# Global attention rows over 18 key blocks, fewer warm-up products and an earlier mask in an attention and two-MoE kernel

## The chip, the cores and the metric

The kernel runs on one core of a Trainium2 chip. A time is the device time of one execution in microseconds (us); the time that counts is the median of several executions. The engines are TensorE (PE, with its weight loads shown apart as PEld), VectorE (DVE), ScalarE (ACT), GpSimd (POOL) and SyncE (SP), which here starts the transfers. Results of TensorE go to PSUM, which the kernel uses as eight banks of 128x512 f32.

## The reference, cut to what matters

```python
# B=4 batches, H=8 heads, Sl=512 local and Sg=32 global rows, D=64
k_all = concat([k_g, k_l], axis=2);  v_all = concat([v_g, v_l], axis=2)
out_g = softmax(q_g @ k_all.T / 8) @ v_all          # every global row sees all 544 keys
mask  = abs(pos[:, None] - pos[None, :]) <= 32      # a local row sees a window
s_l   = concat([q_l @ k_g.T / 8, where(mask, q_l @ k_l.T / 8, -1e9)])
out_l = softmax(s_l) @ concat([v_g, v_l])
x = concat([out_g, out_l]) as (B * 544 = 2176 rows, 512)
x = (silu(x @ w_gate) * (x @ w_val)) @ w_out        # 512 -> 1536 -> 512
h = x @ w_in;  out = (max(h, 0) + alpha * min(h, 0)) @ w_out2      # 512 -> 2048 -> 512
```

## The kernel before

Attention works on units. A `Local` unit is one pair of heads of one batch (16 units); a `Global` unit (L541 to L628) holds the 32 global rows of four heads, so 128 rows, of one batch (8 units, numbered (batch, group)). The 512 local keys are cut into blocks of 32. In `qk` a pair's keys stand as 26 blocks: for two neighbouring blocks of local rows the host writes the three blocks they see, and position `pos(i) = 3*(i//2) + i%2` starts the 128-column window of row block i, so that neighbouring windows overlap and some blocks stand twice. The values `v` stand likewise, 128 rows to each of 16 windows.

A Global unit before takes six windows, `GWIN = (1, 4, 13, 15, 7, 10)`, which cover all keys; blocks that turn up a second time are masked by `gm`. Its steps are: `s`, scores of 6x128 = 768 columns in two PSUM banks (512 and 256), one DVE instruction for each bank that adds the mask, scales and takes the extremum, then one ACT exponential over 768 columns with its sum; `t(0)` and `t(1)`, four and two transposes of 128x128 and one copy each to `pt`; `pv`, 24 products (six windows, four heads) that add up in one bank, and two DVE scalings that write the result twice; `to`, a transpose and two ACT copies.

The MoE matrices are split into a high and a low part, three products for each. The first MoE runs during attention: its gate and value products (`g<-xa,w`, `v<-xa,w`, groups of 12) and output products (`acc<-h,w`). All of this up to about 400 us is recorded by `Planner` (L58 to L272) as atoms, each for one engine. `order` (L207) sorts them: of the atoms that can start it takes the one due first, by estimated costs (`price`), and `flush` (L265) issues them in that order, which is why nearly all rows of that time stand under L272. One engine runs its instructions in the order so found.

At the start four Local units u0 to u3 (batch 0) use all eight banks. From then on attention has only banks a0 and a1, taken by turns (`att_bank`, L391), while the others belong to the MoE products. The order of the start is in L1037 to L1073: SP loads the first pair's `qk` in four parts, then the next pair, the local mask `lm`, the first values; meanwhile `heat(HEAT)` (L399) runs 20 products of 128x128 on a tile of zeros in bank g. Until the first keys have landed TensorE has no other work. Names in the rows: `e` is a unit's scores and later its exponentials, `pt` their transposes, `o` the output before its transposes, `xa` the MoE input, `sg` the silu's factor, `dbl` and `raw` weights on their way to their two parts, `yp` storage that lends itself to the fourth pair of batch 0 (its `qk` and `v`).

Of the kernel before, what the change touches and what calls it, by code (L numbers as in the profile page):

```python
# [28 lines left out]
NPOS = 26  # L29
WIN = 32 * NPOS  # L30
QK = WIN + S + G
GWIN = (1, 4, 13, 15, 7, 10)
NG = len(GWIN)
# [24 lines left out]
class Planner:  # L58
# [121 lines left out]
    def order(self):  # L180
        atoms, preds = self.atoms, self.graph()
        N = len(atoms)
        size = [sum(o.cost for o in a) for a in atoms]
        eng = [a[0].eng for a in atoms]
        before = [sorted({j for e in p.values() for j, _ in e}) for p in preds]
        for i, b in enumerate(before):
            assert not b or b[-1] < i
        after = [[] for _ in atoms]
        for i, b in enumerate(before):
            for j in b:  # L190
                after[j].append(i)
# [12 lines left out]
        table, dma = None, 0.0  # L204
        left = [len(b) for b in before]
        done = [None] * N
        ready = {e: {} for e in self.ENGINES}  # L207

        def data(i):
            t, off = 0.0, 0.0  # L210
            for m, o in enumerate(atoms[i]):
                for j, k in preds[i].get(m, ()):
                    x = done[j][k] - off
                    if eng[j] == eng[i]:
                        x -= atoms[j][k].lat if eng[i] != "sync" else 0.0
# [106 lines left out]
def kernel(  # L322
# [59 lines left out]

    yg = const.tile([128, 4, 128], F32, name="yg")
    lm = attc.tile([128, 4, 128], BF16, name="lm")
    gm = attc.tile([128, 64, 1], BF16, name="gm")[:, 0:4 * NG]
    def bank(tag):
        return ps.tile([128, 512], F32, tag=tag, name="ps_" + tag)

# [7 lines left out]
    zero = attc.tile([128, 128], BF16, name="zero")  # L396
    nc.vector.memset(zero, 0.0)

    def heat(n):  # L399
        t = bank("g")  # L400
        with nc.atom():
            for _ in range(n):
                nc.tensor.matmul(out=t[:, 0:128], lhsT=zero, rhs=zero, start=True, stop=True)


    class Pair:
# [134 lines left out]
    class Global(Unit):  # L541
# [2 lines left out]
            self.pairs = [pairs[b][2 * grp + i] for i in range(2)]  # L544

        def s(self):
            self.sg = attp.tile([128, 1024], F32, tag="e", name="sg")[:, 0:128 * NG]
            self.sm = attp.tile([128, 16], F32, tag="sm", name="smg")[:, 0:1]
            mx = attp.tile([128, 16], F32, tag="mx", name="mxg")
            for part, ws in enumerate((GWIN[0:4], GWIN[4:6])):  # L550
                n = 128 * len(ws)
                s = att_bank()
                with nc.atom():
                    for i in range(0, n, 256):
                        w0, w1 = (32 * pos(w) for w in ws[i // 128:i // 128 + 2])
                        for j in range(4):
                            x = self.pairs[j // 2].qk
                            rows = slice(D * (j % 2), D * (j % 2) + D)
                            step = w1 - w0
                            if step >= 128:  # L560
                                srcs = [(x[rows, w0:w0 + 2 * step].rearrange("p (a c) -> p a c", a=2)[:, :, 0:128], 0)]
                            else:
                                srcs = [(x[rows, w0:w0 + 128], 0), (x[rows, w1:w1 + 128], 128)]
                            for r, d in srcs:
                                dst = s[32 * j:32 * j + 32, i + d:i + d + 256 // len(srcs)]
                                nc.tensor.matmul(
                                    out=dst.rearrange("p (a c) -> p a c", c=128) if len(srcs) == 1 else dst,
                                    lhsT=x[rows, WIN + S:QK],
                                    rhs=r,
                                    start=True,  # L570
                                    stop=True,
                                )
                nc.vector.tensor_tensor_reduce(
                    out=self.sg[:, 512 * part:512 * part + n].rearrange("p (b c) -> p b c", c=32),
                    in0=s[:, 0:n].rearrange("p (b c) -> p b c", c=32),
                    in1=gm[:, 16 * part:16 * part + n // 32].to_broadcast([128, n // 32, 32]),
                    scale=-0.125,
                    scalar=3e38,
                    op0=ALU.add,
# [6 lines left out]
            )  # L586

        def t(self, h):
            if h == 0:
                self.pt = attp.tile([128, 1024], F32, tag="pt", name="ptg")  # L590
            t = att_bank()
            c0, c1 = (0, 512) if h == 0 else (512, 128 * NG)
            with nc.atom():
                for i in range(c0, c1, 128):
                    nc.tensor.transpose(t[:, i - c0:i - c0 + 128], self.sg[:, i:i + 128], ident)
            evac(self.pt[:, c0:c1], t[:, 0:c1 - c0], cp())
            if h == 1:
                self.rc = rc = attp.tile([128, 16, 1], F32, tag="rc", name="rcg")[:, 0]
                nc.vector.tensor_scalar(out=rc, in0=self.sm, scalar1=1e-9, scalar2=None, op0=ALU.add)
                nc.vector.reciprocal(out=rc, in_=rc)  # L600

        def pv(self):
            o = att_bank()
            with nc.atom():
                for i, w in enumerate(GWIN):
                    for j in range(4):
                        nc.tensor.matmul(
                            out=o[32 * j:32 * j + 32, 0:D],
                            lhsT=self.pt[:, 128 * i + 32 * j:128 * i + 32 * j + 32],
                            rhs=self.pairs[j // 2].v[:, j % 2, w],  # L610
                            start=(i == 0),
                            stop=(i == NG - 1),
                        )
            rc = self.rc
            self.o = attp.tile([128, 8, D], F32, tag="o", name="og", bufs=1)
            for h in range(2):
                nc.vector.tensor_scalar(
                    out=self.o[:, h], in0=o[:, 0:D], scalar1=rc, scalar2=None, op0=ALU.mult
                )

        def to(self):
            t = att_bank()
# [957 lines left out]
```

## Time and profile before

| what | value |
|---|---|
| device time, median of 3 runs | 884.55 us (884.41 to 884.82) |
| time of the profiled execution | 886.36 us |
| its span, first to last instruction | 884.6 us |
| mean granted TensorE clock | 0.997 |
| busy share of PE, DVE, ACT | 98%, 78%, 60% |

The profiled execution is one of its own, 1.81 us longer than the median. A row of the timeline gives the start and the length of a group of like instructions, then engine, line, operation, `output<-inputs`, shapes, the count, and in brackets the idle time ahead of it on its engine and what ended that. An f32 product of a tile is recorded as two instructions, so that the 16 score products of a Global unit are `x32`.

### The profile page before, as it was taken

Reading aid. Unit: us, or ns where it says so; the run is one execution under the profiler, and the core shown is the slowest. Engines: PE = TensorE matmul, PEld = TensorE weight load, DVE = VectorE, ACT = ScalarE, POOL = GpSimd, SP = SyncE. Lnnn points to the kernel's source line nnn. Section 1 sums busy time; section 2 is a strip of 40 time slices with the busy share of each in tenths; the row PEclk is TensorE's granted clock in tenths of the full one; section 3 lists DMA queues with packets and bytes.
Section 4 is the critical chain, followed back from the end, with each engine's and each line's share of the span. In section 5 each row is a group of like instructions: output and inputs, shape, how many; then the busy total and the mean of one; then the engine's idle time right before and its main releaser. Section 6 shows DMA issues by size and latency. Waiting matters only on the chain.

```text
span 884.6 us, 17317 instructions
## 1 busy us (share of the span) xinstructions
PE 864.1 (98%) x6868; PEld 749.6 (85%) x6868; DVE 690.8 (78%) x1441; ACT 527.2 (60%) x1051; POOL 0.7 (0%) x6
## 2 busy tenths in 40 slices
PE   5899999999999999999999999999999999999997
PEld 4677778888788787778999999889999889999996
DVE  3997989989877856597666687777896777977776
ACT  5899999878686786654333346343545434554442
POOL 0000000000000000000000000000000000000000
PEclk9999999999999999999999999999999999999999
DMA  8799989899969899975566576455474645585631
GB/s 346 290 408 414 359 340 377 328 361 386 405 261 334 293 343 329 371 291 171 167 234 228 202 256 243 167 219 209 171 285 186 245 183 202 227 293 212 280 143 60
DMA packets 41665, 239.30 MB, mean 271 GB/s; under 512 B 4848, under 2 KB 5488, under 8 KB 19312
## 3 DMA queue, kind: packets, MB, share of 16 engines
q1 hardware_dynamic: 41584, 238.19, 71.5%
q8 instruction: 54, 0.88, 0.4%
q14 instruction: 27, 0.22, 0.1%
HBM read 183.38 MB, written 54.79 MB: 269 GB/s over the span
## 4 chain that ended last, share of the span: by engine, by line
PE 88%; DMA 6%; DVE 2%; ACT 2%; issue 1%; SPq 0%; ACTq 0%; DVEq 0%
PE ps_acc L1450 21%; PE acc L272 10%; PE g L272 10%; PE v L272 10%; PE ps_g L1239 9%; PE ps_v L1239 9%; PE ps_a L1239 8%; PE a L272 7%; PE ps_acc L1296 3%; DMA w2so<-dbl 2%; PE ps_a L1296 2%; DMA dbl<-in_w_dram 2%; DMA qk<-in_qk_dram 1%; DMA yp<-in_w_dram 1%; DMA hring<-w1ss1v 1%
## 5 line engine op out<-in xcount | busy, mean ns | idle before, releaser
L1450 PE MATMUL ps_acc<-w,hring 128*128 128x512 f32 x816 | 194.2, 391 | 0.0
L1450 PEld LDWEIGHTS ps_acc<-w,hring 128*128 128x128 f32 x816 | 152.1, 188 | 30.0 <-ACT hring L1419 0.3
L272 PE MATMUL g<-xa,w 128*128 128x512 f32 x432 | 107.5, 397 | 3.0 <-ACT sg L272 2.2
L272 PE MATMUL v<-xa,w 128*128 128x512 f32 x432 | 106.9, 396 | 0.0
L272 PE MATMUL acc<-h,w 128*128 128x512 f32 x432 | 106.1, 394 | 0.0
L1414 ACT ACTIVATE r<-c 128x384 f32<-128x384 f32 (+1 forms) x96 | 47.8, 498 | 93.2 <-DVE c L1247 93.2
L1455 DVE TENSOR_TENSOR oacc<-ps_acc,oacc 128x512 f32<-128x512 f32 x119 | 81.8, 690 | 22.0 <-PE ps_acc L1450 20.7
L272 PEld LDWEIGHTS g<-xa,w 128*128 128x128 f32 x432 | 79.1, 188 | 22.4 <-ACT sg L272 3.3
L272 PEld LDWEIGHTS acc<-h,w 128*128 128x128 f32 x432 | 79.8, 188 | 18.6 <-issue 1.8
L272 PEld LDWEIGHTS v<-xa,w 128*128 128x128 f32 x432 | 79.3, 188 | 18.3 <-issue 1.4
L1419 ACT ACTIVATE hring<-g 128x384 fp32r<-128x384 f32 (+1 forms) x96 | 48.6, 506 | 55.8 <-DVE g L1416 55.5
L1420 DVE TENSOR_TENSOR hring<-g,hring 128x384 fp32r<-128x384 f32 (+1 forms) x96 | 51.1, 532 | 18.9 <-ACT hring L1419 16.1
L272 ACT ACTIVATE e<-e,mx 128x128 f32<-128x128 f32 (+1 forms) x136 | 57.2, 423 | 13.7 <-DVE mx L272 13.5
L1416 DVE SCALAR_TENSOR_TENSOR g<-g,nal,r 128x384 f32<-128x384 f32 (+1 forms) x96 | 56.7, 591 | 10.6 <-ACT g L1415 10.0
L272 ACT ACT_TABLE_LOAD x46 | 59.0, 1283 | 5.3 <-PE g L272 3.8
L1415 ACT ACTIVATE g<-c 128x384 f32<-128x384 f32 (+1 forms) x96 | 47.9, 499 | 13.7 <-DVE hring L1420 13.7
L1239 PE MATMUL ps_v<-xa,w 128*128 128x320 f32 (+1 forms) x288 | 53.1, 319 | 0.6 <-ACT p L1255 0.5
L1239 PE MATMUL ps_g<-xa,w 128*128 128x320 f32 (+1 forms) x288 | 53.4, 318 | 0.2
L1239 PE MATMUL ps_a<-w 128*128 128x384 f32 (+1 forms) x288 | 51.4, 326 | 0.0
L1239 PEld LDWEIGHTS ps_v<-xa,w 128*128 128x128 f32 x288 | 46.9, 188 | 2.2 <-ACT p L1255 0.7
L1239 PEld LDWEIGHTS ps_g<-xa,w 128*128 128x128 f32 x288 | 47.1, 188 | 1.9 <-DVE u L1263 0.4
L1239 PEld LDWEIGHTS ps_a<-w 128*128 128x128 f32 x288 | 47.9, 188 | 0.1
(209 smaller groups left out, 1397.7 us busy)
## 6 DMA issues: line engine op xcount, KB each, us to landing
dbl<-in_w_dram SPq DMA_DIRECT2D x28, 1024.0 KB, 7.6
w<-w2so SPq DMA_DIRECT2D x24, 1024.0 KB, 5.8
w<-w2sx SPq DMA_DIRECT2D x24, 1024.0 KB, 4.8
w<-w2ss SPq DMA_DIRECT2D x24, 1024.0 KB, 6.6
v<-in_v_dram SPq DMA_DIRECT2D x15, 1024.0 KB, 10.8
qk<-in_qk_dram SPq DMA_DIRECT2D x14, 688.0 KB, 9.5
w2sx<-dbl SPq DMA_DIRECT2D x8, 1024.0 KB, 6.8
w2so<-dbl SPq DMA_DIRECT2D x8, 1024.0 KB, 8.7
```

Source lines behind the costliest of these rows:

```text
L272: last[o.eng] = getattr(getattr(self.nc, o.eng), o.op)(*o.args, **o.kw)
L1239: nc.tensor.matmul(out=o[:, 0:n], lhsT=left(name, a, k), rhs=x[name][:, b, k, 0:n], start=(i == 0), stop=(i == 5),)
L1296: mm = nc.tensor.matmul(out=o, lhsT=a, rhs=x, start=(first and e == 0 and not second), stop=((j, f, e) == (NF1 // 2 - 1, 0, 2) and i not i ...
L1414: nc.scalar.activation(out=rr, in_=u, func=ACTF.Relu)
L1415: nc.scalar.activation(out=g, in_=u, func=ACTF.Relu, scale=-1.0)
L1416: nc.vector.scalar_tensor_tensor(out=g, in0=g, scalar=nal[:, i:i + 1], in1=rr, op0=ALU.mult, op1=ALU.add)
L1419: nc.scalar.activation(out=hi, in_=g, func=ACTF.Copy)
L1420: nc.vector.tensor_tensor(out=lo, in0=g, in1=hi, op=ALU.subtract)
L1450: nc.tensor.matmul(out=o, lhsT=a, rhs=x, start=(i == 0), stop=(i == 5))
L1455: nc.vector.tensor_tensor(out=oacc[tb], in0=o, in1=oacc[tb], op=ALU.add)
```

## The change

The global rows take each key block once. Of the 26 positions, the first two of each group of three hold 16 different blocks (`x[rows, 0:768]` seen as 8 groups of 96, of each the first 64 columns), and the last two positions hold the remaining two: 18 blocks, 576 columns, in parts of 512 and 64. Scores are one product for each head and part, 8 instead of 16. The transposes of a unit go from six to five: four as before, and one over columns 448 to 576, of which the lower 64 rows are copied. The value product cannot use whole windows any more, since a pair of blocks is either the upper or the lower 64 rows of a window: it is done in two halves, even groups on rows 0 to 63 (16 products) and odd groups on rows 64 to 127 (20 products), each in its own bank, taken by `att_bank`; one scaling of the first bank and one scale-and-add of the second put them together. `HEAT` goes from 20 to 4. The second part of the first pair and the mask `lm` are one atom, and `order` now prices each transfer of a SyncE atom for itself.

```diff
-    SLACK=60.0, LOOK=0.1, SWITCH=4.0, MARGIN=0.5, HEAT=20, ND=3, NR=3, LAG=6,
+    SLACK=60.0, LOOK=0.1, SWITCH=4.0, MARGIN=0.5, HEAT=4, TINY=0, ND=3, NR=3, LAG=6,
+GHALF = [(4 * (g // 2) + g % 2, g % 2) for g in range(8)] + [(NB - 2, 1)]
+GLAST = 32 * (pos(NB - 2) + 2)
...
             if e == "sync":
-                dma = max(dma, y + 0.3) + atoms[i][0].lat
-                done[i] = [dma + 1.9]
-                y += 0.45
+                for o in atoms[i]:
+                    dma = max(dma, y + 0.3) + o.lat
+                    done[i].append(dma + 1.9)
+                    y += o.cost
...
-            for part, ws in enumerate((GWIN[0:4], GWIN[4:6])):
+            for part, (c0, n) in enumerate(((0, 512), (512, 64))):
                 s = att_bank()
                 with nc.atom():
+                    for j in range(4):
+                        x = self.pairs[j // 2].qk
+                        rows = slice(D * (j % 2), D * (j % 2) + D)
+                        if part:
+                            dst, r = s[32 * j:32 * j + 32, 0:64], x[rows, GLAST:GLAST + 64]
+                        else:
+                            dst = s[32 * j:32 * j + 32, 0:512].rearrange("p (a c) -> p a c", c=64)
+                            r = x[rows, 0:96 * 8].rearrange("p (a c) -> p a c", a=8)[:, :, 0:64]
+                        nc.tensor.matmul(out=dst, lhsT=x[rows, WIN + S:QK], rhs=r, start=True, stop=True)
...
+                nc.tensor.transpose(t[:, 0:128], self.sg[:, 448:576], ident)
+                evac(self.pt[D:2 * D, 512:640], t[D:2 * D, 0:128], cp())
...
         def pv(self):
+            for half in range(2):
+                o = att_bank()
+                parts.append(o)
+                rows = slice(D * half, D * half + D)
+                mine = [(g, w) for g, (w, k) in enumerate(GHALF) if k == half]
+                with nc.atom():
+                    for i, (g, w) in enumerate(mine):
+                        c = 128 * (g // 2)
+                        for j in range(4):
+                            nc.tensor.matmul(
+                                out=o[32 * j:32 * j + 32, 0:D],
+                                lhsT=self.pt[rows, c + 32 * j:c + 32 * j + 32],
+                                rhs=self.pairs[j // 2].v[rows, j % 2, w],
...
+            nc.vector.tensor_scalar(out=part[:, 0], in0=parts[0][:, 0:D], scalar1=rc, scalar2=None, op0=ALU.mult)
+            nc.vector.scalar_tensor_tensor(
+                out=self.o[:, 0:2],
+                in0=parts[1][:, 0:D].rearrange("p (a d) -> p a d", a=1).to_broadcast([128, 2, D]),
...
-        heat(HEAT)
-        nc.sync.dma_start(out=lm, in_=lmask)
-        p0[0].load_qk(1)
+        heat(HEAT, 128)
+        heat(P["TINY"], 32)
+        with nc.atom():
+            p0[0].load_qk(1)
+            nc.sync.dma_start(out=lm, in_=lmask)
         p0[1].load_qk()
```

What moves with it shows in the order of three stretches. On SP at the start, before (`qk_100` is the first pair, 448 and 256 columns its first part, 384 and 288 its second; `qk_101` the second pair):

```order
L272 DMA qk_100<-in_qk_dram 128x448
L272 DMA qk_100<-in_qk_dram 128x384
L272 DMA qk_100<-in_qk_dram 128x288
L272 DMA qk_100<-in_qk_dram 128x256
L272 DMA qk_101<-in_qk_dram 128x1376
L272 DMA lm<-in_lmask_dram 128x512
L272 DMA v_108<-in_v_dram 128x2048
```

and after:

```order
L276 DMA qk_100<-in_qk_dram 128x384
L276 DMA qk_100<-in_qk_dram 128x288
L276 DMA lm<-in_lmask_dram 128x512
L276 DMA qk_100<-in_qk_dram 128x448
L276 DMA qk_100<-in_qk_dram 128x256
L276 DMA qk_101<-in_qk_dram 128x1376
L276 DMA v_108<-in_v_dram 128x2048
```

The mask has moved ahead of the first part of the first pair, whose last transfer is now fifth instead of fourth.

On PE behind the scores of u3 (`acc<-yp_94`, the last of the four Local units of the start), after:

```order
L276 MATMUL acc_126<-yp_94 32x128
L276 MATMUL acc_125<-yp_94 32x128
L276 MATMUL acc_121<-ident,o_130 128x128 x4
L276 MATMUL acc_122<-ident,e_116 128x128 x4
L276 MATMUL a_114<-ident,e_115 128x128 x4
L276 MATMUL v_129<-ident,e_115 128x128 x4
L276 MATMUL g_103<-v_109,pt_124 32x64 x32
L276 MATMUL acc_126<-ident,e_116 128x128 x4
L276 MATMUL a_114<-qk_100 32x64 x2
L276 MATMUL a_114<-qk_101 32x64 x2
L276 MATMUL a_113<-ident,o_130 128x128 x4
```

The rows down to the value product `g_103<-v_109,pt_124` stand in the same order before; the scores behind are Global(0,0)'s, whose short part of 64 columns now goes first, its long part seven rows later.

On PE at the value product of Global(0,1) (`v_110` and `yp_93` are the two pairs' values), before:

```order
L272 MATMUL a_114<-ident,o_130 128x128
L272 MATMUL a_113<-v_110,pt_124 32x64 x2
L272 MATMUL a_113<-yp_93,pt_124 32x64 x2
...
L272 MATMUL a_113<-v_110,pt_124 32x64 x2
L272 MATMUL a_113<-yp_93,pt_124 32x64 x2
L272 MATMUL g_103<-xa,w_137 128x512 x12
L272 MATMUL a_114<-qk_100 32x256 x2
L272 MATMUL a_114<-qk_101 32x256 x2
```

and after:

```order
L276 MATMUL a_113<-ident,o_130 128x128
L276 MATMUL a_114<-v_110,pt_124 32x64 x2
L276 MATMUL a_114<-yp_93,pt_124 32x64 x2
...
L276 MATMUL g_103<-xa,w_137 128x512 x12
L276 MATMUL a_113<-v_110,pt_124 32x64 x2
L276 MATMUL a_113<-yp_93,pt_124 32x64 x2
...
L276 MATMUL a_114<-qk_100 32x512 x2
L276 MATMUL a_114<-qk_101 32x512 x2
L276 MATMUL v_129<-xa,w_137 128x512 x12
L276 MATMUL a_113<-qk_100 32x64 x2
L276 MATMUL a_113<-qk_101 32x64 x2
```

The two halves of the value product stand 12 MoE products apart, the second runs straight into the next unit's long scores, and the short scores stand another 12 products later.

## Rows read from the trace of the kernel before

**Rows 1.** The page, busy time, share of the span and instructions of each engine.
```profile
PE 864.1 (98%) x6868; PEld 749.6 (85%) x6868; DVE 690.8 (78%) x1441; ACT 527.2 (60%) x1051; POOL 0.7 (0%) x6
```

**Rows 2.** Windows: stretch, its length, busy by engine, PEclk, DMA share, GB/s.
```profile
0.00:50.00 50.00, 36.82 (x698) 28.97 (x698) 33.28 (x111) 35.04 (x92) 0.70 (x6) 0.97 0.86 330
50.00:100.00 50.00, 49.37 (x578) 39.05 (x577) 43.33 (x106) 49.68 (x93) 0.00 (x0) 1.00 0.99 395
100.00:150.00 50.00, 49.97 (x661) 39.55 (x661) 46.41 (x111) 49.59 (x105) 0.00 (x0) 1.00 0.93 371
```

**Rows 3.** Waits of PE: us in total, times, the longest.
```profile
PE g L272 <- ACT sg L272: 2.2, 2, 1.3
PE a L272 <- ACT pt L272: 1.0, 2, 0.6
```

**Rows 4.** Timeline of the first 10 us, SP, PE and DVE.
```profile
0.74 2.30 SPq L272 DMA_DIRECT2D qk<-in_qk_dram  x5
0.99 2.32 PE L272 MATMUL g<-zero 128*128 128x128 bf16 x20 [0.99 <-DVE zero L272]
7.77 1.96 PE L272 MATMUL a<-qk 64*32 64x128 f32 x64 [4.47 <-DMA qk<-in_qk_dram]
9.83 0.29 DVE L272 CUSTOM_DVE_ANT_0 e<-a,lm 128x128 f32<-128x128 f32 x1 [8.90 <-PE a L272]
```

**Rows 5.** Timeline around 21 to 23 us, PE, DVE and ACT.
```profile
21.45 0.41 PE L272 MATMUL acc<-yp 64*32 64x128 f32 x3 [3.46 <-issue]
21.89 0.29 DVE L272 CUSTOM_DVE_ANT_0 e<-acc,lm 128x128 f32<-128x128 f32 x1 [4.13 <-PE acc L272]
23.13 0.40 ACT L272 ACTIVATE e<-e,mx 128x128 f32<-128x128 f32 x1 [1.55 <-DVE mx L272]
```

**Rows 6.** The page, a DMA queue: kind, packets, MB, share.
```profile
q8 instruction: 54, 0.88, 0.4%
```

**Rows 7.** The same queue between 17.9 and 21.4 us.
```profile
q8 instruction: 1, 0.02, 1.8%
```

**Rows 8.** Windows: the stretch of 3 us behind that gap.
```profile
22.50:25.50 3.00, 3.00 (x40) 2.67 (x42) 2.97 (x17) 2.37 (x13) 0.00 (x0) 0.50 1.00 418
```

**Rows 9.** Instruction groups by form, DVE on Global scores: busy, mean ns.
```profile
L272 DVE CUSTOM_DVE_ANT_1 e<-a,gm 128x512 f32<-128x512 f32 x8 | 5.5, 684 | 1.6 <-PE a L272 1.6
L272 DVE CUSTOM_DVE_ANT_1 e<-a,gm 128x256 f32<-128x256 f32 x8 | 3.4, 424 | 0.0
```

**Rows 10.** Timeline of PE, runs of score, value, transpose and MoE products.
```profile
46.70 0.82 PE L272 MATMUL a<-ident,e 128*128 128x128 f32 x6
...
61.06 0.88 PE L272 MATMUL a<-v,pt 128*32 128x64 f32 x48
...
71.55 1.03 PE L272 MATMUL a<-ident,e 128*128 128x128 f32 x8
...
79.13 1.54 PE L272 MATMUL a<-qk 64*32 64x256 f32 x32
80.60 1.65 PE L272 MATMUL v<-xa,w 128*128 128x512 f32 x6
...
87.28 1.10 PE L272 MATMUL a<-v,pt 128*32 128x64 f32 x64
...
91.26 1.16 PE L272 MATMUL a<-qk 64*32 64x128 f32 x64
...
153.98 2.88 PE L272 MATMUL acc<-h,w 128*128 128x512 f32 x12
156.70 2.88 PE L272 MATMUL g<-xa,w 128*128 128x512 f32 x12
...
285.78 1.11 PE L272 MATMUL a<-qk 64*32 64x256 f32 x24
286.82 3.03 PE L272 MATMUL acc<-h,w 128*128 128x512 f32 x12
289.78 0.64 PE L272 MATMUL a<-qk 64*32 64x256 f32 x8
```

More of the change, by code (lines that the diff above doesn't have):

```diff
@@ L31 @@
 QK = WIN + S + G
-GWIN = (1, 4, 13, 15, 7, 10)
-NG = len(GWIN)
+NGB = NB + 2
 P = dict(
-    SLACK=60.0, LOOK=0.1, SWITCH=4.0, MARGIN=0.5, HEAT=20, ND=3, NR=3, LAG=6,
+    SLACK=60.0, LOOK=0.1, SWITCH=4.0, MARGIN=0.5, HEAT=4, TINY=0, ND=3, NR=3, LAG=6,
     wr0=0.75, wr2=0.5, wr3=0.75, wr4=0.6, wr5=0.2,
@@ L384 @@
     lm = attc.tile([128, 4, 128], BF16, name="lm")
-    gm = attc.tile([128, 64, 1], BF16, name="gm")[:, 0:4 * NG]
+    gm = attc.tile([128, 64, 1], BF16, name="gm")[:, 0:NGB]
     def bank(tag):
@@ L397, with heat @@
     nc.vector.memset(zero, 0.0)
-    def heat(n):
+    def heat(n, cols):
         t = bank("g")
@@ L402, in heat @@
             for _ in range(n):
-                nc.tensor.matmul(out=t[:, 0:128], lhsT=zero, rhs=zero, start=True, stop=True)
+                nc.tensor.matmul(
+                    out=t[0:cols, 0:cols], lhsT=zero[:, 0:cols], rhs=zero[:, 0:cols], start=True, stop=True
+                )
     class Pair:
@@ L546, in s @@
         def s(self):
-            self.sg = attp.tile([128, 1024], F32, tag="e", name="sg")[:, 0:128 * NG]
+            self.sg = attp.tile([128, 1024], F32, tag="e", name="sg")[:, 0:32 * NGB]
             self.sm = attp.tile([128, 16], F32, tag="sm", name="smg")[:, 0:1]
             mx = attp.tile([128, 16], F32, tag="mx", name="mxg")
-            for part, ws in enumerate((GWIN[0:4], GWIN[4:6])):
-                n = 128 * len(ws)
+            for part, (c0, n) in enumerate(((0, 512), (512, 64))):
@@ L552, in s @@
                 s = att_bank()
                 with nc.atom():
[L554 to L572, printed above, removed]
@@ L573, in s @@
                 nc.vector.tensor_tensor_reduce(
-                    out=self.sg[:, 512 * part:512 * part + n].rearrange("p (b c) -> p b c", c=32),
+                    out=self.sg[:, c0:c0 + n].rearrange("p (b c) -> p b c", c=32),
                     in0=s[:, 0:n].rearrange("p (b c) -> p b c", c=32),
-                    in1=gm[:, 16 * part:16 * part + n // 32].to_broadcast([128, n // 32, 32]),
+                    in1=gm[:, c0 // 32:(c0 + n) // 32].to_broadcast([128, n // 32, 32]),
                     scale=-0.125,
@@ L591, in t @@
             t = att_bank()
[L592 to L597, printed above, removed]
+            if h == 0:
+                with nc.atom():
+                    for i in range(0, 512, 128):
+                        nc.tensor.transpose(t[:, i:i + 128], self.sg[:, i:i + 128], ident)
+                evac(self.pt[:, 0:512], t, cp())
+            else:
+                nc.tensor.transpose(t[:, 0:128], self.sg[:, 448:576], ident)
+                evac(self.pt[D:2 * D, 512:640], t[D:2 * D, 0:128], cp())
                 self.rc = rc = attp.tile([128, 16, 1], F32, tag="rc", name="rcg")[:, 0]
@@ L602, in pv @@
         def pv(self):
[L603 to L613, printed above, removed]
+            parts = []
+            for half in range(2):
[7 more added lines that the diff above has]
+                        for j in range(4):
+                            nc.tensor.matmul(
+                                out=o[32 * j:32 * j + 32, 0:D],
+                                lhsT=self.pt[rows, c + 32 * j:c + 32 * j + 32],
+                                rhs=self.pairs[j // 2].v[rows, j % 2, w],
+                                start=(i == 0),
+                                stop=(i == len(mine) - 1),
+                            )
             rc = self.rc
             self.o = attp.tile([128, 8, D], F32, tag="o", name="og", bufs=1)
[L616 to L619, printed above, removed]
+            part = self.o[:, 2:3]
+            nc.vector.tensor_scalar(out=part[:, 0], in0=parts[0][:, 0:D], scalar1=rc, scalar2=None, op0=ALU.mult)
+            nc.vector.scalar_tensor_tensor(
+                out=self.o[:, 0:2],
+                in0=parts[1][:, 0:D].rearrange("p (a d) -> p a d", a=1).to_broadcast([128, 2, D]),
+                scalar=rc,
+                in1=part.to_broadcast([128, 2, D]),
+                op0=ALU.mult,
+                op1=ALU.add,
+            )
         def to(self):
@@ L1039 @@
         p0[0].load_qk(0)
-        heat(HEAT)
-        nc.sync.dma_start(out=lm, in_=lmask)
-        p0[0].load_qk(1)
+        heat(HEAT, 128)
+        heat(P["TINY"], 32)
+        with nc.atom():
+            p0[0].load_qk(1)
+            nc.sync.dma_start(out=lm, in_=lmask)
         p0[1].load_qk()
@@ L1552 @@
             lmask[32 * c:32 * c + 32, t, 32 * j:32 * j + 32] = np.where(ok, 0.0, NEG)
-    seen, gm = set(), []
-    for w in GWIN:
-        for b in blocks[pos(w):pos(w) + 4]:
-            gm.append(NEG if b[0] == "x" or b in seen else 0.0)
-            seen.add(b)
-    gmask = np.broadcast_to(np.array(gm, np.float32), (128, 4 * NG))
+    gm = [NEG if b[0] == "x" else 0.0 for g in range(8) for b in blocks[3 * g:3 * g + 2]] + [0.0, 0.0]
+    gmask = np.broadcast_to(np.array(gm, np.float32), (128, NGB))
     arrays = {
```

## The prediction

> **What bounds the kernel now.** I read the page's busy shares first, then windows of 50 us, PE's waits, the timeline of the head, and last the runs of PE instructions by which the changed groups are priced. PE is busy 98% of the span [rows 1]. By stretches it is busy 36.82 of the first 50 us, 49.37 of the next and 49.97 of the third [rows 2]: behind about 45 us the time is PE's own work, and only ahead of that is there something to wait for. So an edit counts in full on PE behind 45 us, counts on the path through DMA, DVE and ACT ahead of it, and counts nothing on DVE or ACT later, where PE's work covers it (behind 45 us PE waits for ACT's `sg` and `pt` once each, 0.9 and 0.4 us, the sums of [rows 3] less the longest).
>
> The head, in order: SP starts the first five transfers in 2.30 us, PE does 20 warm-up products from 0.99 for 2.32 us, then stands still 4.47 us until the first pair has landed, and at 7.77 begins u0's scores; DVE's first masked score follows at 9.83, released by PE and not by the mask [rows 4]. Then PE has a gap of 3.46 us up to 21.45 that no semaphore explains ("issue"). It falls three records ahead of the end of u3's scores. DVE, which needs these, is idle 4.13 us, and ACT, next in the chain, 1.55 us [rows 5]. In this gap lies one packet of the queue that carries instructions [rows 7]. There are 54 such packets in all [rows 6], for 2 x 6868 = 13736 products and weight loads on PE [rows 1], 254 for each. I read the gap as PE running out of fetched instructions while the transfers take 418 GB/s right behind it [rows 8].
>
> **The change part by part.** I sum against the profiled execution, 886.36 us (span 884.6 and 1.76 around it), 1.81 above the median of 884.55. A forecast is 886.36 + change - 1.81.
>
> *Head.* (1) The mask now goes ahead of the last part that u0 waits for: at least its 128 KB, 0.31 us at 418 GB/s [rows 8], at most one start of 2.30 / 5 = 0.46 us [rows 4]. I take 0.35, near the bytes, since what follows already queues. The mask itself gains nothing, as DVE waited for PE. (2) 16 warm-up products and their loads go, 32 instructions. The products ran in the 4.47 us wait, so their own time is free. But if a packet holds a fixed number, the fetch gap falls 32 instructions later in the program: behind u3's scores and some 13 of the 16 transposes that stand ahead of `g_103<-v_109,pt_124`. DVE then gets u3's scores without the gap and ACT's 1.55 us go. That ACT is what the head follows there I take from its run without a break up to the gap. Bounds: nothing to 3.46 us; I take 1.55, since behind the chain ACT is next in line. (3) Global score work on DVE: 512 columns 0.684, 256 columns 0.424 [rows 9], so 64 columns 0.424 - 192 x 0.260 / 256 = 0.229, 0.195 less for each of the two units of the head, 0.39. (4) The copy behind `t(1)` shrinks from 256 columns on 128 rows to 128 on 64, and I let the 0.64 us go that PE waits for `pt` [rows 3]. Later units save as much on DVE and ACT, which PE's work hides; without that cover it would be some 0.2 to 0.5 us for a unit. Head: 0.35 - 1.55 - 0.39 - 0.64 = -2.23 us. Bounds: +0.35 when nothing comes of (2) to (4), -5.0 when the PE waits of 3.46, 1.26 and 0.64 all go.
>
> *PE, eight units.* Busy rows of [rows 10]: scores of 256, 512 and 768 columns take 0.64, 1.11 and 1.54 us; by a line between them 576 take 1.22 and 64 some 0.29. An extra run costs more than its row: the 12 MoE products between two short runs take 289.78 - 286.82 = 2.96 us, elsewhere 156.70 - 153.98 = 2.72, and a run's row reaches 0.07 past the next start (79.13 + 1.54 against 80.60), so 0.17 net. Value products: 24 take 0.88 and 32 take 1.10, 0.0275 each; 16 take 0.66, 20 take 0.77, 36 in one run 1.21. These have half the rows (K = 64), a form no row shows: bounds for the 36 are 1.10, if a product on 64 rows is cheaper than one on 128 by a tenth, and 1.21; the Local scores on 64 rows, 1.16 for 32 products, speak for no large gain, so I take 1.15, the middle.
> - Scores: units (0,0) and (3,0) split as before, 1.11 + 0.29 against 1.11 + 0.64: -0.35 each. Contiguous in (0,1), (1,1), (2,1): -0.32 each. Contiguous before, split now in (1,0), (2,0), (3,1): 1.11 + 0.29 + 0.17 - 1.54 = +0.03 each. Sum -1.57. The first units' scores, -0.67, lie in the head where PE waits anyway: -0.90 counts.
> - Value products: in one run in (0,0) and (1,0), +0.27 each. Split by 12 products in six units: 0.66 + 0.77 + 0.17 - 0.88 = +0.72 each, 4.32. Sum +4.86.
> - Three of the second halves run straight into scores, as in the order of Global(0,1), so two runs become one: 0.15 each, -0.45.
> - Transposes: eight take 1.03 and six 0.82, 0.11 for one, eight fewer: -0.88.
>
> Together +2.63 us; bounds by the contiguous pairs and the run price (0.07 to 0.24) some +1.6 to +3.4. The Trainium skill ("TensorEngine Tiling (Array Packing)", Key Properties) says that a change of tiling mode, not of the tile, drains TensorE. The value products go from 128x32 tiles to the 64x32 of the scores, so by that rule the three glued halves change no mode and save a whole run price; the traces show the price of a run as above (0.24 with its surroundings) but not what of it is the mode. By the page the sum would be 3 x 0.09 = 0.27 us lower.
>
> *Sum.* -2.23 + 2.63 = +0.40; 886.36 + 0.40 - 1.81 = **884.95 us**, no change to speak of (0.2%, 1.77 us, is about what a measurement here can tell).
>
> **The rivals.**
> - *B, the head gives back more.* If the gap of 3.46 us disappears behind transfers or the queue of work, and the two waits for ACT (1.26 and 0.64) go with it: 0.35 - 5.36 = -5.01, + 2.63: 882.17 us. For it: the gap is PE's longest wait but one and ACT and DVE stand idle because of it. Against it: ACT has 49.68 busy of 50 us from 50 to 100 [rows 2] and is full from there.
> - *C, the fetch gap comes back on the path, slower.* The gap only moves; where it falls, the transposes and u1's value product feed DVE and ACT just the same. Then nothing of (2) to (4) is gained and the late start stands: +0.35 + 2.63 = +2.98, 887.53 us. It decides when DVE and ACT run dry for 1.55 us or more behind the moved gap. For it: the gap was 3.46 us, and four exponentials of 0.40 us [rows 5] are all that u3 gives ACT for a half. Against it: the work of both halves of u3 is then in front of ACT.
> - *D, the second bank, slower.* The value product needs two of the two banks a0 and a1, and each must have been read out by its last user, the copy of `t(1)` or the scaling. At the mean of PE's waits for `pt`, 1.0 / 2 = 0.5 us [rows 3], in four of the units that have only 12 products (2.72 us) between the halves: +2.0 on the forecast, 886.95. Against it: PE's 12 products are longer than a reading of 512 columns, 0.684 us on DVE [rows 9].
> - *E, the clock.* PE did 20 products ahead of the 4.47 us wait and then did u0's 64 score records in 1.96 us, where the same form takes 1.16 later [rows 4, 10]: what it did before did not keep it at the faster pace. With 4 products the slow stretch could reach to a third group, 0.8 us, and some transposes, 1.0 together: 885.95. The granted clock of 0.50 (1.2 GHz) stands in the trace behind the gap of 3.46 us [rows 8]. By the Trainium skill ("TensorE: Matmul & The Clock Gate", Part 1) the throttled state is the default and activity lifts it, so that taking out warm-up work can only cost; the rows show that at this place there was little to lose.
>
> **How the numbers follow.** Forecast 0.47 (its own range 883.4 to 886.3, from +-0.9 on PE and +-1.2 in the head), B 0.24, C 0.15, D 0.10, E 0.04. Faster by over 0.2% (under 882.78): 0.20 of B and 0.03 of the forecast, 0.23. Slower by over 0.2% (above 886.32): 0.13 of C, 0.07 of D, 0.04 of the forecast and 0.01 of E, 0.25. Within: 0.52. The range goes from 881.9, a little below B's time, to C's, 887.5; the tails past B and C make up the two in ten.
>
> **What would show it.** In the profile after: PE's first scores at 8.0 to 8.3 us; the gap of about 3 us some 26 instructions behind u3's scores, with DVE's idle time before u3's first score gone; PE's waits for `sg` and `pt` before 52 us shorter; at 62 us the same MoE products about 2.2 us earlier than before, at 400 us level or 0.4 us late; the value halves as rows of 0.66 and 0.77 us; 0.29 for the short scores. It is wrong if the gap stands where it stood or a new one of over 1 us appears behind a value half (C, D), if u2's scores take 1.96 us (E), or if PE's idle time before 62 us shrinks by over 4 us (B).

## The result, and the profile after

The changed kernel takes 894.21 us (median of 4 runs, 892.11 to 897.47), the kernel before 884.68 (4 runs, 884.41 to 884.90): ratio 1.011, interval 1.0089 to 1.013. It is 9.5 us slower. The forecast was 884.95, no change to speak of, in a range of 881.9 to 887.5: the measured time lies 6.7 us above that range. The profiled execution took 892.11 us with a span of 890.3, 5.7 us above that of before, and is the fastest of the four; the others granted a lower mean clock (0.992 to 0.993 against 0.996), which is worth at most some 3 us of their time (an estimate: 0.0035 of 893 us). So the two profiles show 5.7 of the 9.5 us.

The page's engine line (answers to [rows 1]) and the windows (answer to [rows 2], the third 50 us; the two of 3.4 us are the stretches at half clock behind 45 us):

```profile
PE 866.1 (97%) x6908; PEld 746.5 (84%) x6908; DVE 688.9 (77%) x1441; ACT 525.0 (59%) x1049; POOL 0.7 (0%) x6
```

```profile
100.00:150.00 50.00, 49.05 (x654) 38.28 (x653) 45.14 (x111) 48.01 (x89) 0.00 (x0) 0.97 0.86 341
117.80:121.20 3.40, 3.40 (x10) 2.62 (x9) 2.32 (x6) 3.37 (x11) 0.00 (x0) 0.50 0.98 296
302.10:305.50 3.40, 3.24 (x68) 2.79 (x68) 1.29 (x2) 3.33 (x6) 0.00 (x0) 0.50 0.82 286
```

DVE and ACT have less to do, as the change intends, and PE's busy time has hardly risen. But PE, which stood still 0.03 us of the third 50 us before, now stands 0.95, and its clock is 0.50 in two stretches of 3.4 us, where before there was none between 26 us and the end. PE's waits from 52 to 420 us (answer to [rows 3]):

```profile
PE a L276 <- ACT pt L276: 3.7, 4, 2.9
PE v L276 <- DVE t L276: 1.0, 1, 1.0
PE a L276 <- ACT y L276: 0.7, 1, 0.7
PE a L276 <- ACT yp L276: 0.7, 1, 0.7
PE acc L276 <- DVE h L276: 0.4, 1, 0.4
```

That is 6.5 us by this list; before, the waits in the same stretch were 1.3. The head, on the other hand, gave back what was forecast. PE's timeline there, and the last row of ACT's `e` ahead of PE's second wait (answers to [rows 4, 5]):

```profile
6.35 1.96 PE L276 MATMUL a<-qk 64*32 64x128 f32 x64 [4.75 <-DMA qk<-in_qk_dram]
...
21.53 0.49 PE L276 MATMUL v<-ident,e 128*128 128x128 f32 x3 [1.80 <-ACT e L276]
...
23.57 0.32 PE L276 MATMUL a<-qk 64*32 64x64 f32 x8
...
27.80 0.48 PE L276 MATMUL acc<-v,pt 128*32 128x64 f32 x20 [1.05 <-issue]
```

```profile
20.96 0.19 ACT L276 ACTIVATION_READ_ACCUMULATOR e<-e,mx 128x1 f32 x1
```

The first scores start 1.42 us earlier than before, not 0.35 later. The first MoE product stands at 32.28 us instead of 34.33; one execution says little here, since in the profiles of the 16 kernels below with the same changes in the head it stands between 31.57 and 34.05. The gap of 3.46 us stands where the prediction moved it: before, PE does 349 products ahead of it, and after, where 16 of them are gone, the 349 end one product into the last four of the 16 transposes, and there PE stands 1.80 us. The view puts this to ACT's `e`, but the last of these ended at 21.15, 0.38 us before PE went on. A further gap of 1.05 us, with no releaser, follows 128 products on. So the gap has not gone, it is shorter; how much of the 1.80 us is the fetch of instructions and how much ACT stays open. Two groups of rows show what came later, PE's timeline at Global(1,0)'s value product, and at the output transpose of Global(2,1) with a Local unit's value product behind it:

```profile
115.31 0.65 PE L276 MATMUL a<-v,pt 64*32 64x64 f32 x32
116.63 0.76 PE L276 MATMUL a<-v,pt 64*32 64x64 f32 x40 [0.67 <-ACT yp L276]
117.32 4.60 PE L276 MATMUL acc<-h,w 128*128 128x512 f32 x12
```

```profile
295.98 2.98 PE L276 MATMUL v<-xa,w 128*128 128x512 f32 x12
301.82 0.33 PE L276 MATMUL a<-ident,o 128*128 128x128 f32 x1 [2.86 <-ACT pt L276]
302.31 1.93 PE L276 MATMUL a<-v,pt 128*32 128x64 f32 x64 [0.16 <-ACT pt L276]
304.22 3.65 PE L276 MATMUL g<-xa,w 128*128 128x512 f32 x12
```

In the first the second half stands 0.67 us for its bank, and the 12 MoE products behind, 2.88 us elsewhere [rows 10], take 4.60 at half clock. In the second PE waits 2.86 us for that Local unit's copies to `pt`. Why ACT is late there stands in ACT's and SP's timelines:

```profile
297.98 1.12 ACT L276 ACTIVATE raw<-dbl 128x1024 f32<-128x1024 f32 x1 [9.46 <-DMA dbl<-in_w_dram]
299.12 1.28 ACT L276 ACT_TABLE_LOAD   x1
300.42 0.77 ACT L276 ACTIVATE e<-e,mx 128x576 f32<-128x576 f32 x1
...
301.19 1.06 ACT L276 ACTIVATE pt<-a 128x512 f32<-128x512 f32 x2
```

```profile
279.81 0.33 SPq L276 DMA_DIRECT2D v<-in_v_dram  x1
280.55 0.32 SPq L276 DMA_DIRECT2D w2so<-dbl  x1
...
288.93 0.33 SPq L276 DMA_DIRECT2D dbl<-in_w_dram  x1
```

ACT stands 9.46 us in front of the first step of a weight conversion, with the exponential of Global(3,0) behind it. The weights were sent for at 288.93, once the store `w2so<-dbl` had emptied the buffer; the store was queued on SP behind a load of `v`, which waited for PE's second half (279.02 to 279.78) of Global(2,1)'s value product to let go of the values. The sum of the profiled executions: head's idle time 13.8 us in both, PE's gaps that end between 52 us and the end of the first MoE 5.5 against 1.3, time lost in the half-clock stretches there 3.3 against none (half of PE's busy time in them), the rest 1.8 less: +5.7 us.

### The profile page after: what moved, and what is told of

Its sections match the earlier page's. It is cut to its first block, busy times and chain, and to the rows that moved or that the text cites. A ratio compares the mean times of both kernels' runs of the same rounds, so it can differ in the third digit from the quotient of the medians.

```text
span 890.3 us, 17376 instructions
## 1 busy us (share of the span) xinstructions
PE 866.1 (97%) x6908; PEld 746.5 (84%) x6908; DVE 688.9 (77%) x1441; ACT 525.0 (59%) x1049; POOL 0.7 (0%) x6
## 4 chain that ended last, share of the span: by engine, by line
PE 73%; DMA 10%; ACT 8%; DVE 6%; issue 1%; SPq 1%; ACTq 0%; DVEq 0%
PE ps_acc L1463 21%; PE ps_g L1252 9%; PE ps_v L1252 9%; PE ps_a L1252 8%; PE acc L276 6%; PE g L276 6%; PE v L276 5%; DMA dbl<-in_w_dram 4%; PE a L276 4%; PE ps_acc L1309 3%; PE ps_a L1309 2%; DMA w2so<-dbl 2%; ACT e L276 1%; ACT L276 1%; DVE y L276 1%
## 5 line engine op out<-in xcount | busy, mean ns | idle before, releaser
L276 PE MATMUL acc<-h,w 128*128 128x512 f32 x432 | 108.1, 400 | 0.4 <-DVE h L276 0.4
L1468 DVE TENSOR_TENSOR oacc<-ps_acc,oacc 128x512 f32<-128x512 f32 x119 | 81.8, 691 | 22.1 <-PE ps_acc L1463 20.9
L1428 ACT ACTIVATE g<-c 128x384 f32<-128x384 f32 (+1 forms) x96 | 47.9, 499 | 13.6 <-DVE hring L1433 13.5
```

The source lines that it names most:

```text
L276: last[o.eng] = getattr(getattr(self.nc, o.eng), o.op)(*o.args, **o.kw)
L1428: nc.scalar.activation(out=g, in_=u, func=ACTF.Relu, scale=-1.0)
L1468: nc.vector.tensor_tensor(out=oacc[tb], in0=o, in1=oacc[tb], op=ALU.add)
```

## The experiments

All were timed beside runs of the kernel before; a time is a median, the ratio is to the kernel before. They form five series (1 to 4, 5 to 8, 9 to 12, g, h), in which the kernel before has medians from 884.25 to 885.57 us, so a difference between two series is better read from the ratios. Where an order is said to be kept, the list of atoms to issue stands in the kernel as a table (`PLAN`) instead of the planner's own:

```diff
-        for i in self.order():
+        for i in PLAN:
```

**1 to 4. Which part, and are six runs the price?**

```diff
 e3: before,      HEAT=20 -> HEAT=4
 e1: before,      HEAT=4, the mask's atom and the planner's pricing as in the change
 e2: the change,  HEAT=20, mask and load_qk(1) as before
 e4: the change,  one nc.atom() around both halves of pv instead of one around each
```

> The head's part of the change alone (4 warm-up products, mask in one atom with the first pair's second part, transfers of an atom priced singly) on the global rows of before. Behind the head its order is that of before nearly row for row. Theory 'order' (the loss of 9.5 us comes from the new order of all engines that the global part brings, by waits on ACT and DVE and the half-clock stretches behind them): this part keeps what the head gives back, 882 to 884 us. Theory 'work' (the loss is the global part's own PE work): the same. Theory 'head' (4 products are too few, or the earlier mask delays): slower than before, 887 us or more.

883.52 us (ratio 0.9985, 0.997 to 0.9999): faster by some 1.2 us, barely clear of no difference. "Head" falls.

> The global rows' part alone, with 20 warm-up products and the mask where it was. Theory 'order': slower than before by the 2.6 us of PE work and by waits of a new order of its own, 888 to 897 us, with PE waits behind 45 us at other places than after the whole change. Theory 'work': slower by the loss after the change and what the head gave there, 9.5 + 2 us, 896 us, with hardly any PE waits behind 45 us. Theory 'head': 887 us or less.

891.99 (1.0081, 1.0057 to 1.0104). The loss is the global part's. With 20 products the fetch gap is back (3.2 us "issue").

> The kernel before with 4 warm-up products instead of 20 and nothing else; the order of all engines is that of before but for the 16 products. If the instruction packets hold a fixed number, the fetch gap (3.46 us at 17.99) moves 32 instructions on, behind u3's scores, and DVE and ACT no longer stand still for u3: 1.5 to 2.5 us less, 882 to 883 us. If the gap stays where it is: 884.6 us. Theory 'head': slower, 886 us or more, with the granted clock back to full later than 12.24 us.

884.15 (0.9993, 0.998 to 1.0007): the gap has moved, as in the change. Behind the same 349 products PE stands 1.66 us, put to ACT's `e`, which had ended 0.94 us before PE went on, and 0.64 us ("issue") 128 products later. What the move gives back is no more than 1.8 us and can't be told from nothing, nor from e1's gain, so that the mask's place is not shown to give anything.

> The changed kernel with the two halves of a value product in one atom, so that they stand together in one run of 36 products. Theory 'work': six runs fewer, about 0.45 us each, 2.7 us less: 891.5 us. Theory 'order': the order of the rest changes again, so that the time follows the PE waits behind 45 us and the half-clock stretches, and not the 2.7 us: anything from 885 to 897 us.

884.99 (1.0013, 0.9991 to 1.0035): 9.2 us less than the change, three times the six runs, so the runs' price is not the cause.

**5 to 8. The order, or the work?**

```diff
 e5: the change,  PLAN = each atom at its counterpart's place in e1's order
 e6: e1's work,   PLAN = each atom at its counterpart's place in the changed kernel's order
 e7: the change,  its own order, one ACT atom (raw<-dbl at 297.98) behind e of Global(3,0) and the two pt copies
 e8: as e5,       each second half behind the next group of 12 MoE products
```

> All of the changed kernel's work, but issued in the order of the kernel before (with the head's part): each atom stands where its counterpart stood, both halves of a value product where the one stood, so in one run. Theory 'order': 883.5 us of the head's part alone, scores -1.6, transposes -0.9, eight value products in one run +0.3 each: about 883.5 us, between 882 and 886. Theory 'work': no better than with the halves in one run in an order of its own, less nothing, and if the halves cost what the changed kernel lost, 889 us or more.

895.47 (1.0119, 1.0099 to 1.014). Against "order".

> The reverse: the work of the kernel before (with the head's part; six windows, six transposes, 24 products), issued in the order of the changed kernel. Theory 'order': it loses most of what the changed kernel lost, 889 to 894 us, with PE waits at the same places (118 us, 300 us). Theory 'work': 883 to 885 us, as with the head's part alone.

884.62 (0.9998, 0.9982 to 1.0014). "Order" falls: the old work in the new order loses nothing. But "work" as PE time doesn't explain e4.

> The changed kernel with one atom moved: ACT's first step of a weight conversion, which waited 9.46 us for its transfer at 297.98 us, stands behind the exponential and the two copies of Global(3,0) instead of ahead of them. Theory 'order': PE's wait of 2.86 us at 301.8 and the half-clock stretch at 302.1 (1.7 us) go, 4 to 5 us less than the changed kernel: 889.5 us. Rival: the conversion is needed as soon, and the wait turns up behind it: 893 to 895 us.

891.16 (1.007, 1.0049 to 1.0091): 3 us less. PE's wait did turn up behind, for `sg`, 3.4 us at 299 us: the rival, in part. The two copies that the expectation gives to Global(3,0) are a Local unit's.

> As the replay of the old order, but in all eight units the second half of the value product stands one MoE group of 12 products behind the first. By the prices of the prediction a split costs 0.45 us: 3.6 us more than the replay, 887 us. Rival 1: MoE products between the halves hide the cost, the same time as the replay. Rival 2: the half-clock stretches come with split halves, 6 us or more above the replay.

889.27 (1.0047, 1.0028 to 1.0065): 6 us less than with the halves in one run, the opposite of every expectation. Contiguous halves wait for something that halves apart don't. The waits name it: in e5 PE waits 5.2 us for ACT's `y` and `yp`, the copies of a unit's output out of the other bank; in e8 0.3.

**9 to 12. The second bank, and the values held.** New theory: what the second half needs, not what it does, costs the time. In e9 and e10 the work and order are e1's, with one thing changed in the value product.

```diff
 e9:  24 products in one run, out = (bank 1 if i < 3 else bank 2), then scale, scale and add
 e10: one bank, windows 0-2 and 3-5 in two atoms, the second behind the next 12 MoE products
 e11: the change, its own order, second half right behind the first
 e12: the change, its own order, on SP each later load of v two transfers further back
```

> The work of the kernel before with the head's part, in that kernel's order (883.5 us), but the 24 products of a global unit's value product, still on 128 rows and in one run, go to two banks, windows 0 to 2 to one and 3 to 5 to the next, and are scaled and added as in the changed kernel. Theory 'second bank' (a unit takes a0 and a1 seven times instead of six, and the value product waits in front for ACT to have read the bank of the transposes just ahead): PE waits on ACT's y and yp as in the replay (5 us, and half-clock stretches behind), 891 to 895 us. Theory 'rows' (products on 64 rows cost the time): 883 to 885 us.

894.36 (1.0116, 1.0074 to 1.0158), with products on 128 rows, old scores, old transposes. PE's waits from 52 to 420 us, then the value product of one unit:

```profile
PE a L335 <- ACT y L335: 4.9, 2, 2.9
PE a L335 <- ACT yp L335: 2.4, 2, 1.5
```

```profile
380.48 0.60 PE L335 MATMUL a<-ident,o 128*128 128x128 f32 x4
381.00 0.54 PE L335 MATMUL a<-v,pt 128*32 128x64 f32 x24
384.49 0.54 PE L335 MATMUL a<-v,pt 128*32 128x64 f32 x24 [2.94 <-ACT y L335]
```

The four transposes of the output fill one bank, the first half the other, and the second half stands 2.94 us until ACT has copied the transposes. "Rows" falls: the second bank alone makes this loss in the old order (10.8 us above e1, 11.6 by the ratios).

> The same order and work, one bank for a value product, but its 24 products in two runs of 12 with one MoE group between them in all eight units. Price of a split by the prediction 0.17 + 0.2 us of busy time, 8 x 0.4 = 3 us, 886.5 us. Theory 'values held' (the split keeps the value tiles in use 3 us longer, SP's load of the next ones waits and all transfers queued behind it): more than that, 888 us or more, with SP waiting longer for PE in front of loads of v. If the split is free: 883.5 us.

889.53 (1.0066, 1.0044 to 1.0088), 6 us above e1: more than the 3 us put on the runs. SP's waits for PE's `a` products from 52 to 420 us go from 22.1 to 37.5 us, as "values held" has it. But of the difference between the two profiles (5.5 us) 1.85 lie ahead of the first MoE product, where no product is split yet, so this run alone does not decide.

> The changed kernel in its own order, but each second half of a value product right behind the first. Theory 'values held': the loads of v no longer wait, ACT's idle time at 297.98 us falls from 9.46 to some 4.6 us as in the control with the old work, and PE's 2.86 us wait with the half clock behind it goes: 888 to 890 us, less what the second bank then costs. Theory 'second bank': the waits move in front of the second halves and cost at least as much, 892 us or more.

892.76 (1.0092, 1.0064 to 1.012). PE's wait at 299 us is gone, but PE waits 3.0 us for ACT's `y` and `yp`: both waits come and go as the theories have it. That their prices nearly cancel is argued from the time, not shown.

> The changed kernel in its own order on PE, ACT and DVE; only on SP each load of v (of the later batches) stands two transfers later, behind those that need not wait for the second half. Theory 'values held': SP's waits for PE in front of v go, the weight load at 288.93 us is issued 3 us earlier, PE's 2.86 us wait at 301.8 and the half clock behind it go: 889 to 890 us against 894.2. If the time stays at 893 to 895, the late loads are not what holds ACT up.

892.38 (1.0091, 1.0065 to 1.0117). The weights are sent for at 284.90 instead of 288.93, and the wait at 301.8 and every half-clock stretch behind 45 us are gone: the late loads do make that wait. But the time falls by 1.8 us only, not by 4 to 5; a wait of 1.9 us at 312.8 has come.

**13 to 18. In the changed kernel's own order.** All but g4 keep the work of e1 and the order of e6 (884.62 us).

```diff
 g1: 12 + 12 products on 128 rows in two banks, where the change has its halves
 g2: the same in one bank
 h1: as g2, only Global(2,1)'s value product split
 h2: as g2, all split as there but Global(2,1)'s
 h3: as g2, on SP each later load of v two transfers further back
 g4: the change, halves in one atom, w.pv() ahead of x.to() in apump, planned anew
```

> The work of the kernel before (with the head's part) in the order of the changed kernel, as in the control that took 884.6 us, with one thing more: the value product's 24 products on 128 rows go in two halves of 12 to two banks, at the places where the changed kernel has its halves. Scores and transposes are those of before. Theory 'second bank and split': this alone brings the changed kernel's time, 891 to 895 us, with PE waits on ACT's yp, pt and y at the same places. Theory 'columns' (the short scores and the new transposes upset the order): 884 to 887 us.

893.69 (1.0105, 1.0088 to 1.0122): the changed kernel's time without its scores, its transposes and its 64-row products. "Columns" falls.

> As the one with two banks, but both halves add up in one bank, so that a unit takes six banks as before and only the split is left: the value tiles are held until the second half. Theory 'values held': SP's loads of v wait for PE, 888 to 892 us. Theory 'second bank': 885 to 887 us, the runs' price of 0.2 to 0.4 us for each of six splits alone.

891.98 (1.0084, 1.0069 to 1.0099): the split alone brings 7.4 of the 9.5 us (7.6 by the ratios), the second bank another 1.7, though the intervals of the two overlap.

> The old work in the changed kernel's order, one bank, and only the value product of Global(2,1) split by one MoE group; the other seven stand in one run. Theory 'values held': this split alone makes the load of v at 277 us, the store behind it and the weight load at 287 us late, and with them ACT's idle time of 9.8 us and PE's 3.6 us at 297 us: 889 to 891 us against 884.6 with no split and 892.0 with six. Rival (each split costs its own run): 884.6 + 0.4 = 885 us.

891.57 (1.007, 1.0047 to 1.0093): one split does nearly all, 7.0 us above e6 (6.4 by the ratios). The same rows of e6 and of h1, SP, PE and ACT; e6 first:

```profile
273.67 0.33 SPq L335 DMA_DIRECT2D v<-in_v_dram  x1
277.78 0.32 SPq L335 DMA_DIRECT2D w2so<-dbl  x1
...
284.26 0.33 SPq L335 DMA_DIRECT2D dbl<-in_w_dram  x1
```

```profile
272.76 0.88 PE L335 MATMUL a<-v,pt 128*32 128x64 f32 x48
...
276.47 2.88 PE L335 MATMUL g<-xa,w 128*128 128x512 f32 x12
```

```profile
290.37 1.15 ACT L335 ACTIVATE raw<-dbl 128x1024 f32<-128x1024 f32 x1 [4.62 <-DMA dbl<-in_w_dram]
```

and h1:

```profile
277.35 0.33 SPq L335 DMA_DIRECT2D v<-in_v_dram  x1
278.86 0.32 SPq L335 DMA_DIRECT2D w2so<-dbl  x1
...
287.40 0.33 SPq L335 DMA_DIRECT2D dbl<-in_w_dram  x1
```

```profile
273.35 0.54 PE L335 MATMUL a<-v,pt 128*32 128x64 f32 x24
...
276.78 0.54 PE L335 MATMUL a<-v,pt 128*32 128x64 f32 x24
277.25 3.03 PE L335 MATMUL g<-xa,w 128*128 128x512 f32 x12
...
300.67 0.33 PE L335 MATMUL a<-ident,o 128*128 128x128 f32 x1 [3.66 <-ACT pt L335]
...
303.07 5.49 PE L335 MATMUL g<-xa,w 128*128 128x512 f32 x12 [0.81 <-ACT sg L335]
```

```profile
296.68 1.12 ACT L335 ACTIVATE raw<-dbl 128x1024 f32<-128x1024 f32 x1 [9.84 <-DMA dbl<-in_w_dram]
```

From the start of the value product to the second MoE group behind it e6 takes 3.71 us (272.76 to 276.47) and h1 3.90, so the split costs 0.19 us by itself, and PE in h1 is 0.8 us behind e6 at 277 us, 0.6 of it from earlier. The load of `v`, held by the second half at 276.78, is 3.68 us behind, the weights' load 3.14, ACT's conversion 6.3. The load of `v` and the transfers behind it now come close together, and they take longer: the store 8.5 us from issue to landing for 6.5 in e6, the weights 9.2 for 6.0. PE is 8.5 us behind at 312: a wait of 3.66 us, another of 0.81, and 12 MoE products in 5.49 us instead of 3.0 are what follows from a split of 0.19.

> The reverse: all splits of the changed kernel but that of Global(2,1). Theory 'values held': PE's wait at 297 us and the half clock behind it are gone, 886 to 888 us. Rival: five sixths of the loss stay, 890.5 us or more.

887.22 (1.0018, 0.9999 to 1.0036): the other five splits together cost 2.6 us (1.8 by the ratios). Their own price is 0.8 us of it (0.13 to 0.23 each, by the same count as in h1); the rest are small waits.

> All splits, one bank, and on SP each load of v of the later batches stands two transfers later. Theory 'values held, and SP's queue with them': the weight load is issued at 284 us again, PE's wait at 297 us goes, 886 to 888 us; waits for the values themselves may come instead, since they are now loaded later. If the queue is not what holds the weights up: 891 to 893 us.

891.25 (1.0064, 1.0046 to 1.0082). PE's wait at 297 us is gone, with no half clock behind 45 us, as the theory has it, yet the time is but 0.7 us below g2's (1.8 by the ratios): against the forecast. In its profile PE is 2.5 us behind e6 at the first MoE product already. From that product to the end of the span the profiles take 850.1 us (e6), 852.4 (h2), 854.2 (h3), 857.2 (h1), 858.0 (g2, and the changed kernel) and 860.5 (g1). Counted so, moving the loads of `v` gives back 3.8 of g2's 7.9 us, a little less than the 4 to 6 of the forecast, and what is left is splits of 0.13 to 0.23 and new waits, the longest 1.0 us for `pt` at 314.5. Whether the head is late in all of h3's runs one profile can't show: why its median is no lower stays open.

> The changed kernel with both halves of a value product in one atom, recorded ahead of the output transposes of the unit before instead of behind them, so that its two banks are those of the two transposes t(0) and t(1) it must wait for anyway; all planned anew. If the second bank's wait is what costs, 881 to 885 us, at or below the one with the halves together (885.0) and below the kernel before; if the wait then moves to the output transposes, 886 us or more.

888.44 (1.0052, 1.0032 to 1.0072). In this kernel a unit's output is overwritten by the next unit's before it is transposed, so part of the attention output is not the reference's; the time stands for the order alone. Not faster than e4: the waits moved, as its second case has it.

Not tried: halves on 64 rows in one bank, and a fourth buffer for the values.

## Why the prediction was wrong, step by step

- *"behind about 45 us the time is PE's own work", so that an edit "counts nothing on DVE or ACT later".* This step failed. It is a fact about the old schedule, not about the change: PE's idle time from 52 us to the end of the first MoE went from 1.3 to 5.5 us, and 3.3 us more were lost at half clock behind the waits. The prediction put these waits at nothing (or, as rival D, at 2.0 us with a chance of 0.10). It also read the old rows too well: of the waits that it calls "once each" behind 45 us, `pt` has a second, the 0.64 us that end at 50.9, which it counts to the head.
- *The split value product, "+0.72 each".* As PE work it was priced too high, and the loss is not there. From the first half to the MoE product behind the second the changed kernel takes 0.56, 0.55 and 0.64 us more than e6 where a half stands alone (a wait of 0.72 taken off) and 0.28 to 0.29, scores included, where the second half runs into scores: 2.6 us for the six, where the sum has 4.32 - 0.45. The sum charges the 12 MoE products between the halves with 0.24 us more than elsewhere; at Global(2,0) they take 2.98 us, and behind the one run of e6 2.89 already. What was left out is what the second half holds: the value tile, for one MoE group longer, and behind it SP's load, the store and the weight load queued there, ACT's conversion and the exponential behind that. In h1 one split costs 7 us (6.4 by the ratios) this way, and in e12 and h3, where the loads of `v` stand elsewhere, the wait at that place is gone, though little of the time came back. The prediction named what waits on PE, but not who waits for the tile that PE reads.
- *Rival D, the second bank: right in kind, "+2.0".* In the changed kernel's order g1 - g2 = 1.7 us, near that, if not clear of noise. It was argued away with the 12 products between the halves; in the old order, without them, the same bank costs 10.8 us (e9 - e1).
- *Transposes, scores: right.* The short scores take 0.32 us (0.29 forecast). Without them the loss is the same (g1), and e4 has them and is as fast as before.
- *Head, -2.23.* The timelines agree (-2.05 at the first MoE product), the runs give 1.2 us (e1), within the bounds of +0.35 and -5.0; with a spread of 2.5 us between executions the agreement to 0.2 us is partly luck. Term (1) had the wrong sign, -1.42 for +0.35 in this profile, but the mask is not shown to be the reason: e2, with the mask in its old place, starts its first scores at 6.09 us. Term (2)'s gap moved to the place that was forecast and shrank, from 3.46 to 1.80 us, with 1.05 us more 128 products on.
- *Rivals C and E:* the gap did come back behind u3's scores, as C had it, but shorter, and the head gained even so; the slow scores did reach to u2 (0.42 us each at 13.5 us), as E had it, but hidden in the head.

The rule of the Trainium skill on tiling modes ("TensorEngine Tiling (Array Packing)", Key Properties) would have moved the sum by 0.27 us. In the traces a second half that runs into scores costs some 0.3 us less than one that stands alone, nearer to the whole price of a run, 0.24, than to the 0.15 of the sum, but the scores there changed their shape as well, so no run here tells.

## What to carry to other kernels

A price list of the instructions that an edit adds is half an estimate; the other half is, for every tile and bank that they touch, until when it is held and which queue stands behind its next user. Ask this of in-order queues above all (SP's transfers, ACT behind a conversion that waits for one): in h1 a load that waited 3.7 us held up a store and a weight load behind it that had nothing to do with it. And a schedule in which waits were hidden before does not hide them for another kernel: replaying the old work in the new order showed in one run that the order alone costs nothing, and adding one property at a time to the old work (a bank, a split) finds the one that matters. The head's part alone (e1, ratio 0.9985, at most 0.9999) is the one part that is not slower.

## What the runs showed of the hardware that was not expected

A wait can cost PE more than its length, but need not: behind 0.67 us for a bank (116.0) the granted clock was 0.50 for 3.4 us and 12 products took 4.60 us for 2.88, behind 3.66 us (h1) 5.49. Behind waits of 1.04 us (50.6) and 0.72 us (382.9) in the changed kernel, and of 1.93 us in e12 (312.8), it stayed at 1.00. What tells the two cases apart is not shown.

And the gap that the prediction read as PE's fetch of instructions follows the count of instructions: in all 20 profiles PE stands still behind its first 349 products, whatever the next one is. With 20 warm-up products that is inside u3's scores (3.46 us before, 3.23 in e2), with 4 inside the transposes, 0.2 to 2.6 us, where the view names ACT. In most of the latter a second gap, "issue", of 0.5 to 1.9 us stands 128 products later.
